# Where tiles live and who loads them: an earlier q, earlier half swaps and SyncE row loads in a planned kernel

## The chip, the cores and the metric

The kernel runs on one core of a Trainium2 chip. The metric is the device time of one execution in microseconds; the figure given is the median of five runs. A profile of one execution shows what each engine did: PE (TensorE matmuls, with PEld for its weight loads), DVE (VectorE), ACT (ScalarE), POOL (GpSimd, here the issuer of DMAs and little else) and SP (SyncE, which only issues DMAs).

## The reference, cut to what matters

Two independent branches share one output: columns 0 to 1023 are a long convolution, columns 1024 to 2047 a diagonal state-space recurrence. Sequence length S is 2048, width D is 1024, everything comes and goes as bf16.

```python
# branch A
k_shift = sum(k_pad[:, t:t+S, :] * shift_k[:, ks-1-t] for t in range(4))
kv = k_shift * v
y  = irfft(rfft(pad(kv, 2*S)) * rfft(pad(ssm_k, 2*S)))[:S]     # along S
a  = q * (y + kv * ssm_D)
# branch B
Bu = einsum("bld,pd->blp", x, B_bar)                           # complex
h[t] = Lam_bar * h[t-1] + Bu[:, t]                             # 2048 steps
b  = 2 * einsum("blp,dp->bld", h, C).real + x * Dskip
out = concatenate([a, b], -1)
```

## The kernel before

The whole work is one list of 1684 named steps, `ORDER`, written out by hand (or by a planner) in the source. Every step is a small function; each engine issues its own instructions in the order of the list, and semaphores between engines are put in automatically. A step that needs a tile buffer which an earlier tile still holds makes its first writer wait. So the list sets the order on each engine, and waits come from data, from buffers and from DMA landings.

**Branch B** works in 16 chunks i of 128 time steps.
- `xl`, `x`: load and transpose x. `bl.j.w` loads a tile of B (256 KB), `bT` transposes it on PE, `bc` copies it into `BT` (ACT for w = 0, DVE for w = 1). `cl`, `cT`, `cc`, `cx` do the same for C. `tab`, `sin`, `stt` and others build rotation tables.
- `U.i.p` (L468): 32 matmuls of 128 columns each, a quarter of x·B for chunk i; `ue.i.p` evicts on ACT.
- `r1`, `r2` (rotate and add, L480 and L489), `ca`, `sc` (two scans, L500), `cm`, `cy` (carry to the next chunk), `r3`, `r4`: the recurrence, all on DVE. Chunks follow each other through the carry.
- `y.i.h.part` (L524, L529): h·C and the skip term, on PE; `ye` evicts, `yst` stores; the last chunk is stored in halves by `ysh`.

**Branch A** does the FFT as three matmul stages with the data passed through DRAM.
- `k.r` and `v.n` load rows of k and v; `kvm`, `kva`, `kvb`, `kvc` (L569 to L587) make the shifted product on DVE for 16 row sets. `am` (PE), `ae` (ACT), `ast` (POOL) transform and store it to `Ys_kv`.
- `hl`, `hd`, `hT`, `hc`, `hm`, `he`, `hst` do the same for the filter, in four quarters, to `Ys_h`. This is the h stage; its tiles are `hT` and `ysbh`.
- The middle stage has 32 groups g, two in one load: `lh`, `l` load the filter's and the data's groups (512 KB each), `lw` the weights; `sh`, `sk` are matmuls (L674); `she` and `ske` evict to `hab` and `x16`. `sw.g` swaps the two halves of 64 partitions of `hab` with two DMAs from POOL (L701, L702), `pr.g` multiplies on DVE (L707), `sa` is the inverse matmul (L716), `sae` evicts and `vst` stores two groups to `Vs`.
- The last stage has 16 row sets n: `vl.n` loads two tiles `vv` from `Vs` (L734), `ql.n` a tile of q (L739), `a3` matmul (L746), `a3e` evict, `qm` multiply by q (L765), `ost` store; the last three row sets use `qp` and half stores `oth`.

Branch A's tiles of the stages live in three pools that follow each other in the same space: `a1` (rows and h stage), `a2` (the 32 groups), `a3` (last stage). The first tile of a pool closes the pool before:

```python
        if name not in pools:
            for o in list(cms):
                cms.pop(o).__exit__(None, None, None)
            cms[name] = tc.tile_pool(name=name, bufs=1)
```

So the first q tile, in `a3`, has to wait until every tile of `a2` that shares its space is free, the last `vsb` among them. `vv` has 7 buffers, `qt` 6, `hab` 4, `l2k` 3. The rows `k.-3` to `k.0` and `v.0` are loaded by POOL (`k.-3` to `k.-1` in two parts each, 112 and 15 rows), the other rows by SP.

Of the kernel before, what the change touches and what calls it, by code (L numbers as in the profile page):

```python
# [15 lines left out]
BF16 = mybir.dt.bfloat16  # L16
# [8 lines left out]
def a_constants():  # L25
# [12 lines left out]
    for si in range(4):  # L38
# [23 lines left out]
CFG = dict(nx=3, mt=2, u=3, xT=6, h=2, yo=2, ps_t=2, ps_u=2, ps_y=1, ps_a=3, kr=8, ld=5, acc=2, ysb=3, hk=3,  # L62
           hT=2, ysbh=2, l2=3, wts=4, swa=0, x16=4, hab=4, vsb=2, vv=7, qt=6, ot=5, bdve=8)
# [3 lines left out]
xl.0 xl.1 ld_F xl.2 bl.5.0 ld_par ld_w bl.1.1 bl.0.0 bl.3.0 k.-3 bl.0.1 bl.6.1 xt.0 k.-2 bl.1.0 bl.6.0 xt.1 x.0 bl.4.0  # L67
k.-1 bl.3.1 x.1 lw.0 par_T wb.0 bl.2.0 k.0 p32 bT.1.1 bl.4.1 ld_G exp1 bl.2.1 lw.1 v.0 wb.1 bc.1.1 bl.7.1 xt.2 wbe.0
hl.0.1 dve2 k.1 wbe.1 bT.5.0 dve3 x.2 tab.0 wb.4 bl.5.1 bc.5.0 bT.3.0 sm_pre x.4 exp2 wb.2 wbe.4 bT.0.1 bc.3.0 tab.1
lw.2 lw.3 dd wbe.2 x.3 bT.0.0 sin0 wb.3 wb.5 bc.0.1 wb.6 k.2 k.3 tab.2 bc.0.0 hl.0.0 bT.1.0 bc.1.0 par_rest bT.6.1  # L70
bl.7.0 wbe.6 U.0.0 x.5 wbe.3 wbe.5 tab.3 sin.2 bc.6.1 wb.7 U.1.0 hl.1.0 wbe.7 tab.4 k.4 z1.2 kvm.0 ue.0.0 bT.3.1
bT.6.0 sin.4 U.2.0 cl.0.1 ue.1.0 bc.3.1 z1.1 kva.0 bT.7.1 bc.6.0 bc.7.1 z1.0 bT.2.1 kvb.0 bT.4.0 ue.2.0 bc.2.1 bc.4.0
kvc.0 bT.4.1 eo.0 kvm.1 bT.2.0 v.2 am.0.0 v.1 am.0.1 am.0.2 bc.2.0 ae.0.2 U.0.1 bc.4.1 ae.0.0 eo.1 stt.0 am.0.3 ae.0.1
kvm.2 U.1.1 ae.0.3 ast.0.0 ue.0.1 ast.0.1 eo.2 bT.5.1 stt.1 U.2.1 cl.2.0 ue.1.1 k.5 bc.5.1 eo.3 bT.7.0 hd.0 kva.1
U.0.2 ue.2.1 cl.0.0 bc.7.0 stt.2 U.2.2 ue.0.2 kva.2 stt.3 U.0.3 ue.2.2 kvb.1 z2 kvb.2 cT.0.1 kvm.3 ue.0.3 U.1.2 cl.3.1
cc.0.1 cx.4.1 U.2.3 ue.1.2 kvc.1 cx.7.1 r1.0 cT.2.0 ue.2.3 U.1.3 cc.2.0 kvc.2 r2.0 cl.1.1 U.3.0 ue.1.3 cx.5.0 kva.3
k.6 cT.0.0 sc.0 ue.3.0 cl.1.0 am.1.0 U.3.1 cl.3.0 cc.0.0 cx.7.0 ae.1.0 am.1.1 cx.5.1 hT.0.0 ue.3.1 am.1.2 ae.1.1
am.1.3 U.3.2 hc.0.0 ast.1.0 k.7 v.3 ae.1.2 kvb.3 cx.4.0 ae.1.3 cm.0 cT.1.0 r3.0 ue.3.2 ast.1.1 cT.3.1 cc.1.0 am.2.0
am.2.1 cl.2.1 U.3.3 cc.3.1 kvm.4 ae.2.0 ae.2.1 cT.1.1 ue.3.3 hm.0.0.0 ast.2.0 am.2.2 v.4 cc.1.1 hT.0.1 v.5 r4.0
hm.0.0.1 he.0.0.0 he.0.0.1 kvc.3 hm.0.0.2 hT.0.2 ae.2.2 hst.0.0.0 r1.1 hc.0.1 hm.0.0.3 am.2.3 he.0.0.2 cT.3.0 he.0.0.3  # L80
v.8 cc.3.0 kva.4 hst.0.0.1 U.4.0 v.7 hc.0.2 r2.1 ae.2.3 U.4.1 ue.4.0 cy.0 ast.2.1 kvb.4 ca.1 kvm.5 cT.2.1 ue.4.1
hm.0.1.0 hT.0.3 cc.2.1 hm.0.1.1 hm.0.1.2 hl.1.1 U.4.2 he.0.1.0 kvm.6 cx.6.1 he.0.1.1 he.0.1.2 hst.0.1.0 cx.6.0
hm.0.1.3 y.0.0.0 ue.4.2 kvc.4 he.0.1.3 sc.1 am.3.0 hc.0.3 hl.2.0 U.4.3 hst.0.1.1 k.8 k.9 ae.3.0 v.6 v.9 am.3.1 y.0.0.1
ue.4.3 ae.3.1 hm.0.2.0 am.3.2 ast.3.0 hm.0.2.1 he.0.2.0 y.0.0.2 ae.3.2 kva.5 he.0.2.1 am.3.3 am.4.0 ae.3.3 am.4.1
hst.0.2.0 kva.6 y.0.0.3 ae.4.0 ae.4.1 hm.0.2.2 ye.0.0 cm.1 ast.3.1 kvb.5 he.0.2.2 ast.4.0 hd.1 r3.1 hT.1.0 hm.0.2.3
am.4.2 y.0.1.0 he.0.2.3 hc.1.0 hst.0.2.1 y.0.1.1 kvc.5 ae.4.2 r4.1 am.4.3 hT.1.1 x.6 ae.4.3 hm.0.3.0 y.0.1.2 kvb.6
he.0.3.0 ast.4.1 cy.1 r1.2 am.5.0 k.10 y.0.1.3 k.11 ae.5.0 v.12 hm.0.3.1 hT.1.2 ye.0.1 hm.0.3.2 he.0.3.1 hm.0.3.3
yst.0 kvc.6 he.0.3.2 U.5.0 hst.0.3.0 he.0.3.3 r2.2 hc.1.1 kvm.7 hst.0.3.1 U.5.1 ue.5.0 am.5.1 am.5.2 ue.5.1 ca.2 k.12
kva.7 hm.1.0.0 y.1.0.0 ae.5.2 ae.5.1 kvm.8 hT.1.3 ast.5.0 hm.1.0.1 he.1.0.0 U.5.2 hl.2.1 he.1.0.1 hst.1.0.0 sc.2 k.13
am.5.3 hl.3.0 hm.1.0.2 ue.5.2 hm.1.0.3 U.5.3 he.1.0.2 he.1.0.3 ae.5.3 hst.1.0.1 hc.1.2 y.1.0.1 ue.5.3 ast.5.1 am.6.0  # L90
y.1.0.2 ae.6.0 kvb.7 am.6.1 am.6.2 kva.8 hm.1.1.0 ae.6.1 ae.6.2 hm.1.1.1 ast.6.0 y.1.0.3 r3.2 he.1.1.0 he.1.1.1 am.6.3
hm.1.1.2 ye.1.0 hst.1.1.0 hm.1.1.3 ae.6.3 y.1.1.0 hc.1.3 kvc.7 ast.6.1 hm.1.2.0 cm.2 kvb.8 y.1.1.1 he.1.1.2 he.1.1.3
r4.2 am.7.0 hst.1.1.1 y.1.1.2 x.7 ae.7.0 hd.2 kvc.8 hT.2.0 y.1.1.3 r1.3 he.1.2.0 hT.2.1 ye.1.1 hm.1.2.1 hm.1.3.0
hm.1.3.1 he.1.2.1 yst.1 cy.2 kvm.9 U.6.0 hst.1.2.0 he.1.3.0 he.1.3.1 am.7.1 hst.1.3.0 U.6.1 ue.6.0 r2.3 k.14 ae.7.1
v.11 v.13 ast.7.0 kva.9 v.10 am.7.2 y.2.0.0 ue.6.1 ca.3 ae.7.2 kvm.10 hm.1.2.2 hm.1.2.3 y.2.0.1 he.1.2.2 he.1.2.3
U.6.2 hc.2.0 hst.1.2.1 sc.3 k.15 am.7.3 hm.1.3.2 ue.6.2 hm.1.3.3 y.2.0.2 ae.7.3 he.1.3.2 ast.7.1 U.6.3 hc.2.1 he.1.3.3
kvb.9 hst.1.3.1 am.8.0 am.8.1 ue.6.3 kva.10 hm.2.0.0 y.2.0.3 ae.8.0 ae.8.1 am.8.2 kvc.9 he.2.0.0 hT.2.2 ast.8.0 r3.3
ye.2.0 am.8.3 hm.2.0.1 ae.8.2 y.2.1.0 ae.8.3 he.2.0.1 ast.8.1 am.9.0 y.2.1.1 ae.9.0 cm.3 hst.2.0.0 kvb.10 am.9.1 r4.3
am.9.2 x.8 y.2.1.2 ae.9.1 ae.9.2 ast.9.0 kvc.10 hm.2.0.2 hm.2.0.3 hm.2.1.0 he.2.0.2 r1.4 y.2.1.3 he.2.0.3 hc.2.2
hT.2.3 hst.2.0.1 hm.2.1.1 hm.2.1.2 hl.3.1 ye.2.1 v.15 kvm.11 he.2.1.0 U.7.0 yst.2 he.2.1.1 hst.2.1.0 am.9.3 y.3.0.0  # L100
ue.7.0 r2.4 ae.9.3 y.3.0.1 he.2.1.2 ast.9.1 kva.11 hm.2.1.3 U.7.1 cy.3 hc.2.3 hd.3 ca.4 kvb.11 he.2.1.3 kvm.12 am.10.0
hst.2.1.1 am.10.1 ue.7.1 y.3.0.2 ae.10.0 ae.10.1 am.10.2 am.10.3 sc.4 hT.3.0 ae.10.2 ast.10.0 hm.2.2.0 ae.10.3
# [12 lines left out]
am.14.3 y.5.0.1 ae.14.2 ae.14.3 r2.6 am.15.3 U.9.0 ast.14.1 ae.15.3 lh.0 ast.15.1 lh.1 ca.6 sc.6 U.9.1 ue.9.0 U.9.2
ue.9.1 l.1 l.0 U.9.3 lh.2 ue.9.2 r3.6 l.2 y.5.0.2 ue.9.3 cm.6 sh.0.0 sh.0.1 r4.6 y.5.0.3 she.0.0 she.0.1 sh.1.0 cy.6
r1.7 sh.1.1 ye.5.0 sw.0 sh.2.0 lh.3 she.1.0 y.5.1.0 she.1.1 she.2.0 sw.1 sh.2.1 sh.3.0 she.2.1 U.10.0 she.3.0 sw.2
sk.2.0 sk.0.0 ue.10.0 y.5.1.1 ske.2.0 ske.0.0 sk.0.1 sk.1.0 x.11 y.5.1.2 ske.0.1 ske.1.0 pr.0 sk.1.1 sk.2.1 y.5.1.3
ske.1.1 ske.2.1 sa.0.0 ye.5.1 r2.7 sh.3.1 sa.0.1 sae.0.0 lh.4 yst.5 y.6.0.0 she.3.1 pr.1 sae.0.1 sw.3 sk.3.0 sk.3.1
y.6.0.1 ske.3.0 pr.2 l.3 ske.3.1 l.4 sa.1.0 ca.7 y.6.0.2 sc.7 sae.1.0 sh.4.0 sa.1.1 she.4.0 sk.4.0 y.6.0.3 sae.1.1  # L120
ske.4.0 lw.5 vst.0 sa.2.0 ye.6.0 sh.4.1 sk.4.1 sae.2.0 U.10.1 ske.4.1 she.4.1 pr.3 sw.4 sh.5.0 sh.5.1 ue.10.1 r3.7
y.6.1.0 lh.5 she.5.0 she.5.1 sa.2.1 sh.6.0 sw.5 sh.6.1 sae.2.1 y.6.1.1 cm.7 she.6.0 r4.7 she.6.1 sa.3.0 x.12 sk.5.0
# [53 lines left out]
def full_kernel(ctx, tc, A_q, A_k, A_v, A_shift_k, A_ssm_k, A_ssm_D, B_x, B_Lre, B_Lim, B_Bre, B_Bim,  # L176
                B_Cre, B_Cim, B_log_dt, B_Dskip, out, cfg=None):
    c = dict(CFG)
    c.update(cfg or {})
    nc = tc.nc  # L180
    P = 128
# [59 lines left out]
    def ap_pool(name):  # L241
        if name not in pools:
            for o in list(cms):
                cms.pop(o).__exit__(None, None, None)
            cms[name] = tc.tile_pool(name=name, bufs=1)
            pools[name] = cms[name].__enter__()
        return pools[name]
# [582 lines left out]
```

## Time and profile before

| | |
|---|---|
| median of five runs | 388.63 us (387.83 to 391.05) |
| the profiled execution's own time | 388.94 us |
| its span | 387.0 us |
| PE busy | 360.8 us |
| DVE busy | 329.5 us |
| ACT busy | 279.3 us |
| POOL busy | 128.2 us |
| DMA traffic | 101 MB, 261 GB/s on average |
| granted PE clock | 0.998 |

The span runs from the first to the last instruction; the execution's own time has 1.9 us more around it. Matmuls are pipelined, so PE's busy time says that PE had work in flight, not that it ran at its peak. [...] An engine's idle time counts only where that engine, or one that waits for it, sets the end.

### The profile page before, as it was taken

The page shows a single profiled execution, that of the slowest core. Times are in us where ns is not written, and L with a number is a line of the kernel's source. Part 1 is how long each engine was busy: PE and PEld are TensorE (multiplying, and loading weights), DVE is VectorE, ACT ScalarE, POOL GpSimd, SP SyncE. Part 2 cuts the span into 40 slices and gives each one's busy share as a digit, 9 for nine tenths or more (in the row PEclk, how much of TensorE's full clock was granted, in tenths as well). Part 3 has the DMA queues.
Part 4 walks back from the last instruction along what each step waited for, and adds up shares of the span by engine and source line. Part 5 has one row for each costly group of instructions (what it writes and reads, how often), then busy time and mean ns, then how long its engine had stood idle before and what let it go on. Part 6 is the DMA issues. An engine that isn't in the chain of part 4 may idle for free.

```text
span 387.0 us, 8963 instructions
## 1 busy us (share of the span) xinstructions
PE 360.8 (93%) x3509; PEld 246.9 (64%) x3553; DVE 329.5 (85%) x341; ACT 279.3 (72%) x511; POOL 128.2 (33%) x223
## 2 busy tenths in 40 slices
PE   3998998999999998999979999989998999999995
PEld 2687997859586775778536465555554676864442
DVE  2999999999999999999387999995853694989944
ACT  3799579787868698974857789868997876245331
POOL 7001003445555447661323234322343331011220
PEclk9999999999999999999999999999999999999999
DMA  7999399898685936456999999988999643998984
GB/s 241 367 311 336 103 229 338 237 314 282 260 243 192 286 125 217 191 174 211 287 263 262 331 262 305 281 299 269 319 276 276 234 152 135 319 402 278 371 314 164
DMA packets 60506, 101.15 MB, mean 261 GB/s; under 512 B 28451, under 2 KB 31523, under 8 KB 60464
## 3 DMA queue, kind: packets, MB, share of 16 engines
q1 hardware_dynamic: 46512, 58.21, 51.7%
q0 software_dynamic: 13872, 42.35, 30.2%
q8 instruction: 28, 0.46, 0.5%
q14 instruction: 14, 0.11, 0.1%
q10 hardware_dynamic: 80, 0.01, 0.0%
HBM read 53.10 MB, written 33.55 MB: 224 GB/s over the span
## 4 chain that ended last, share of the span: by engine, by line
PE 68%; DMA 12%; DVE 7%; issue 5%; ACT 5%; SPq 2%; POOL 0%; DVEq 0%; ACTq 0%
PE ps_u L468 23%; PE ps_y L524 22%; PE ps_a L716 6%; PE ps_a L674 5%; DMA hab<-hab 4%; DMA CT<-in_B_B_re_dram 4%; PE ps_a L746 3%; PE ps_a L593 2%; PE ps_a L639 2%; PE ps_y L529 2%; DVE mt L480 2%; PE ps_t L617 2%; DMA Ys_h<-ysbh 1%; DVE mt L569 1%; ACT ysbh L647 1%
## 5 line engine op out<-in xcount | busy, mean ns | idle before, releaser
L524 PE MATMUL ps_y<-CT,h 128*128 128x512 bf16 x478 | 130.1, 379 | 2.8 <-ACT yo L539 1.6
L468 PEld LDWEIGHTS <-BT 128*128 128x128 bf16 x2048 | 118.8, 98 | 8.7 <-ACT BT L434 1.3
L468 PE MATMUL ps_u<-xT,BT 128*128 128x128 bf16 x2048 | 123.3, 220 | 0.8 <-ACT BT L434 0.8
L524 PEld LDWEIGHTS <-h 128*128 128x128 bf16 x512 | 46.9, 98 | 47.0 <-issue 0.7
L500 DVE TENSOR_TENSOR_SCAN h<-rtab,h 128x1024 bf16<-128x1024 f32 x32 | 71.5, 2276 | 0.2
L470 ACT CAST u<-ps_u 128x512 bf16<-128x512 f32 x64 | 38.1, 595 | 41.2 <-PE ps_u L468 41.2
L707 DVE TENSOR_TENSOR hab<-x,hab 128x2048 bf16<-128x2048 bf16 x32 | 38.5, 1220 | 23.6 <-ACT vsb L727 11.5
L654 POOL DMA_DIRECT2D Ys_h<-ysbh x64 | 45.4, 713 | 33.5 <-ACT ysbh L647 33.2
L480 DVE TENSOR_TENSOR mt<-u,Z 128x4096 bf16<-128x4096 bf16 x16 | 36.6, 2286 | 10.6 <-ACT u L470 10.6
L727 ACT CAST vsb<-ps_a 128x512 bf16<-128x512 f32 x64 | 36.9, 599 | 10.8 <-PE ps_a L716 7.1
L647 ACT CAST ysbh<-ps_a 128x512 bf16<-128x512 f32 x64 | 36.5, 622 | 8.5 <-DMA Ys_h<-ysbh 5.9
L604 POOL DMA_DIRECT2D Ys_kv<-ysb x32 | 17.8, 557 | 64.8 <-ACT ysb L602 64.4
L602 ACT CAST ysb<-ps_a 128x512 bf16<-128x512 f32 x64 | 36.5, 616 | 3.6 <-PE ps_a L593 3.6
L696 ACT CAST x<-ps_a 128x512 bf16<-128x512 f32 x64 | 36.8, 597 | 3.1 <-PE ps_a L674 2.9
L716 PE MATMUL ps_a<-hab,wts 128*128 128x512 bf16 x122 | 34.8, 379 | 4.2 <-DVE hab L707 4.1
L684 ACT CAST hab<-ps_a 128x512 bf16<-128x512 f32 x64 | 36.4, 600 | 2.1 <-PE ps_a L674 1.9
L701 POOL DMA_DIRECT2D hab<-hab x32 | 16.9, 527 | 61.0 <-ACT hab L684 60.5
L480 DVE TENSOR_TENSOR mt<-h,Z 128x4096 bf16<-128x4096 bf16 x16 | 36.6, 2286 | 0.2
L569 DVE TENSOR_TENSOR mt<-kring,wbc 128x4096 bf16<-128x4096 bf16 (+3 forms) x16 | 30.1, 1883 | 0.0
L539 ACT CAST yo<-ps_y 128x512 bf16<-128x512 f32 x32 | 19.1, 598 | 15.1 <-PE ps_y L524 15.1
L529 PE MATMUL ps_y<-Dd,xT 128*128 128x128 bf16 x128 | 28.0, 219 | 0.6
L639 PE MATMUL ps_a<-hT,F1t 128*128 128x256 bf16 x128 | 21.7, 272 | 1.6 <-ACT ysb L602 0.8
(118 smaller groups left out, 459.0 us busy)
## 6 DMA issues: line engine op xcount, KB each, us to landing
Ys_kv<-ysb POOLq DMA_DIRECT2D x32, 256.0 KB, 3.2
Ys_h<-ysbh POOLq DMA_DIRECT2D x64, 128.0 KB, 3.3
hk<-Ys_h SPq DMA_DIRECT2D x16, 512.0 KB, 6.5
l2k<-Ys_kv SPq DMA_DIRECT2D x16, 512.0 KB, 5.6
hab<-hab POOLq DMA_DIRECT2D x64, 128.0 KB, 4.7
Vs<-vsb POOLq DMA_DIRECT2D x16, 512.0 KB, 5.4
vv<-Vs SPq DMA_DIRECT2D x32, 256.0 KB, 5.4
hk<-in_A_ssm_k_dram SPq DMA_DIRECT2D x8, 512.0 KB, 4.7
```

What stands on the lines that cost most here:

```text
L468: nc.tensor.matmul(pu[:, w, jl, :], BT[:, 2 * jp + jl, w, d, :], xT[:, d, :], start=(d == 0), stop=(d == ND - 1))
L470: E["ue"] = lambda i, jp: nc.scalar.copy(st["u", i][:, :, 2 * jp:2 * jp + 2, :], st.pop(("pu", i, jp))[:])
L480: nc.vector.tensor_mul(m, s_, win(Z))
L500: nc.vector.tensor_tensor_scan(gf[:, a * W:(a + 1) * W], rt1, gf[:, a * W:(a + 1) * W], 0.0, ALU.mult, ALU.add)
L524: nc.tensor.matmul(py[:], h[:, 1 - w, j, :], CT[:, j, w, dh * 512:(dh + 1) * 512], start=(j == 0 and w == 0), stop=(j == NJ - 1 and w == 1))
L602: nc.scalar.copy(st["ysb", n2, cc][:, dh * 512:(dh + 1) * 512], st.pop(("pa", n2, w))[:])
L647: nc.scalar.copy(st["yh", qd, n4, w // 2][:, :, w % 2, :], st.pop(("pa", qd, n4, w))[:].rearrange("p (c d) -> p c d", c=2))
L654: gpd(Ys_h[cc, n0:n0 + 2, :, qd * DQ:(qd + 1) * DQ].rearrange("n k d -> k n d"), t_[:, cc, :, :])
L696: nc.scalar.copy(st["x16", g][:, w * 512:(w + 1) * 512], st.pop(("ps", "l2k", g, w))[:])
L707: nc.vector.tensor_mul(hab[:], st.pop(("x16", g))[:].unsqueeze(1).to_broadcast([P, 2, D]), hab[:])
L716: nc.tensor.matmul(pt[:], st["w", gq][:, gi, 1 + a, :], hab[:, a, w * 512:(w + 1) * 512], start=(a == 0), stop=(a == 1))
L727: nc.scalar.copy(st["vsb", gq][:, gi, w * 512:(w + 1) * 512], st.pop(("ps", "v", g, w))[:])
```

## The change

All 1684 steps are kept, and their list is written anew in another order. The code differs in this:

```diff
-CFG = dict(nx=3, mt=2, u=3, ..., l2=3, ..., hab=4, vsb=2, vv=7, qt=6, ot=5, bdve=8)
+CFG = dict(nx=3, hb=2, mt=2, u=3, ..., l2=3, ..., hab=4, vsb=2, vv=5, qt=6, ot=5, bdve=8)
...
     def ap_pool(name):
         if name not in pools:
-            for o in list(cms):
-                cms.pop(o).__exit__(None, None, None)
-            cms[name] = tc.tile_pool(name=name, bufs=1)
+            if name == "a2k":
+                ap_pool("a2h")
+            dead = {"a2h": ("a1h",), "a2": ("a1",), "a2k": ("a1",), "a3q": ("a2k",), "a3": ("a2",)}.get(name, ())
+            for o in dead:
+                if o in cms:
+                    cms.pop(o).__exit__(None, None, None)
+            cms[name] = tc.tile_pool(name=name, bufs=1, side="left" if name in ("a1", "a2", "a3") else "right")
...
+    def kring():
+        if "kring" not in st:
+            st["kring"] = ap_pool("a1").tile([P, c["kr"], D], BF16, name="kring", bufs=1)
+            nc.vector.memset(st["kring"][0:1, 0:3, :], 0.0)
+        return st["kring"]
...
-        eng = spd if r > 0 else gpd
+        eng = spd
...
-        (spd if n2 else gpd)(st["v", n2][:], vr[:, n2, :])
+        spd(st["v", n2][:], vr[:, n2, :])
...
-        st["hT", qd, n4] = atile("a1", "hT", [P, 4, DQ])
+        st["hT", qd, n4] = atile("a1h", "hT", [P, 4, DQ])
...
-            st["yh", qd, n4, w // 2] = atile("a1", "ysbh", [P, 2, 2, DQ])
+            st["yh", qd, n4, w // 2] = atile("a1h", "ysbh", [P, 2, 2, DQ])
...
-            st[nm, gq] = ap_pool("a2").tile([P, GC, D], BF16, name=nm, bufs=c["l2"])
+            st[nm, gq] = ap_pool("a2k").tile([P, GC, D], BF16, name=nm, bufs=c["l2"])
...
-            st["hab", g] = atile("a2", "hab", [P, 2, D])
+            st["hab", g] = atile("a2h", "hb", [P, 2, D]) if g % 5 < c["hb"] else atile("a2", "hab", [P, 2, D])
...
-        st["qt", n2] = atile("a3", "qt", [P, D])
+        st["qt", n2] = atile("a3q", "qt", [P, D])
```

There are now two stacks of pools. On the left `a1`, `a2` and `a3` follow each other; on the right `a1h` (tiles of the h stage) gives way to `a2h`, two further buffers `hb` for `hab`, and `a2k` (the loaded data groups `l2k`) gives way to `a3q` (the q tiles). Two of five groups take `hb`, so `hab` and `hb` together have six buffers in place of four; `vv` has five in place of seven.

Three places of the new list that are spoken of below. The start, before:

```
xl.0 xl.1 ld_F xl.2 bl.5.0 ld_par ld_w bl.1.1 bl.0.0 bl.3.0 k.-3 bl.0.1 bl.6.1 xt.0 k.-2 bl.1.0 bl.6.0 xt.1 x.0 bl.4.0 k.-1 bl.3.1
```

and after:

```
xl.0 xl.1 ld_w xl.2 k.-3 ld_par bl.1.1 ld_F k.-2 ld_G bl.5.0 bl.1.0 xt.0 bl.0.1 k.-1 xt.1 x.0 bl.7.1 bl.0.0 wb.0 x.1 bl.2.0 par_T
wbe.0 bl.5.1 p32 bT.1.1 bl.3.0 exp1 bl.2.1 xt.2 bl.3.1 bc.1.1 bl.6.0 k.0 ...
```

The first groups, before:

```
lh.0 ast.15.1 lh.1 ca.6 sc.6 U.9.1 ue.9.0 U.9.2 ue.9.1 l.1 l.0 U.9.3 lh.2 ue.9.2 r3.6 l.2 y.5.0.2 ue.9.3 cm.6 sh.0.0 sh.0.1 r4.6
y.5.0.3 she.0.0 she.0.1 sh.1.0 cy.6 r1.7 sh.1.1 ye.5.0 sw.0 sh.2.0 lh.3 she.1.0 ...
```

and after:

```
lh.0 ast.15.1 lh.1 U.9.2 ue.9.1 y.5.0.2 ue.9.2 r3.6 y.5.0.3 l.0 l.1 U.9.3 ye.5.0 lh.2 cm.6 r4.6 y.5.1.0 ue.9.3 cy.6 r1.7 sh.0.0
sh.0.1 sh.1.0 she.0.0 y.5.1.1 she.0.1 she.1.0 sh.1.1 sw.0 sh.2.0 x.11 U.10.0 she.1.1 she.2.0 sw.1 l.2 ...
```

The end of the groups, after (before, the first `ql` and `vl` came behind the last `vst`):

```
ske.31.0 ql.1 U.13.3 ske.31.1 ql.4 pr.29 ql.5 sae.28.1 ql.0 ql.2 ql.6 pr.31 ... sa.31.1 sae.31.0 U.15.0 sae.31.1 r2.13 vst.15
ca.13 y.12.0.2 sc.13 ue.15.0 U.15.1 y.12.0.3 ue.15.1 U.15.2 vl.1 ye.12.0 vl.4 ...
```

## The prediction

> **What bounds the kernel now.** I read the page's engine line first, then busy time by stage, then the chain of waits, and last the single waits at the two pool changes.
>
> ```profile
> span 387.0 us, 8963 instructions
> ...
> PE 360.8 (93%) x3509; PEld 246.9 (64%) x3553; DVE 329.5 (85%) x341; ACT 279.3 (72%) x511; POOL 128.2 (33%) x223
> ```
>
> A busy PE of 93% overstates the work. In the timeline 32 matmuls of `U` take 1.79 us (56 ns each) and four of `y` take 0.86 us (215 ns each). At that pace all PE work (64 `U` pieces of 1.79, 512 `y` matmuls, and so on down the list of steps) adds up to 350.0 us, so 37 us of the span are lost on PE. Setting each step's measured start against the work ahead of it in the order gives where: 16.6 us before `U.0.1` at 32.0, 6.6 more until 155, then 3.0 at `sa.0.0`, 1.0 at `sa.4.0`, 1.3 at `sh.16.1`, 1.3 at `sa.23.0`, 2.1 in four places after 350, and 4.9 behind the last matmul at 382.1. The table by stage (columns PE, PEld, DVE, ACT, POOL) says which engine is the limit of each stage:
>
> ```profile
> 10.00:184.00 174.00, 166.94 (x1998) 132.69 (x2017) 172.43 (x205) 138.15 (x243) 65.94 (x101) 1.00 0.78 245
> 184.00:200.00 16.00, 13.31 (x90) 7.03 (x90) 8.18 (x9) 11.07 (x21) 4.75 (x9) 1.00 1.04 277
> 200.00:320.00 120.00, 116.44 (x914) 68.77 (x929) 97.75 (x78) 99.32 (x193) 40.35 (x76) 1.00 0.89 272
> 320.00:340.00 20.00, 19.89 (x263) 16.00 (x263) 13.85 (x12) 8.60 (x16) 1.08 (x2) 1.00 0.65 235
> 340.00:370.00 30.00, 28.86 (x168) 14.41 (x169) 28.80 (x26) 15.15 (x28) 5.43 (x10) 1.00 0.95 351
> ```
>
> From 10 to 184 **DVE** has 1.6 us of idle time in 174: whatever PE wins there it must give back, because `y` and `am` wait for DVE. From 184 to 340 **PE** is the limit. From 340 to 370 DVE is full again (the recurrence of the last two chunks). The largest single loss of the PE stage is the change of pools at 186:
>
> ```profile
> 184.63 2.20 DVE mt L480
> 186.84 7.59 issue
> 194.62 1.23 DVE hab L707
> 195.90 0.60 PE ps_a L716 x2
> ```
>
> The first product (L707) starts at 194.62, 7.6 us after DVE is free. The view of the tile `hab` between 184 and 200 shows what it waits for: the first swaps, issued at 185.6 and 186.2, are slow to land.
>
> ```profile
> DMA to landing us min/median/max: 7.4/8.2/8.8
> ```
>
> In the quiet stretch from 308 to 320 the same swaps land in 2.2 to 3.6 us. At the other pool change SyncE's queue waits long, but in the timeline PE doesn't: `q` is issued at 328.19, `Vs` rows at 331.13, and the first output matmul starts at 339.84 on time.
>
> ```profile
> SPq L739 <- DMA Vs<-vsb: 17.0, 2, 15.1
> ```
>
> **What the Trainium skill says.** "TensorE: Matmul & The Clock Gate", section "Wait — 56ns, not 53.3ns?", gives 55.6 and 215.7 ns start to start for 128 and 512 columns; the 56 and 215 ns above agree, so PE can't go faster per step. "DMA: Bandwidth & Descriptors", section "Issuing engines are not separate DMA queues", says that loads started by SyncE and GpSimd share the same 16 DMA engines. The trace agrees: swaps of GpSimd take 8.2 us beside SyncE's loads and 2.8 us (median) without. So moving `k`, `v` to SyncE brings no bandwidth, and a swap's price is the traffic beside it.
>
> **The change, part by part.** All 1684 steps stay the same; no arithmetic is added or removed. What changes is the order, who issues eight row loads, and which space tiles take.
>
> (a) *k, v rows on SyncE* (eight loads: six parts of `k.-3` to `k.-1`, `k.0`, `v.0`). POOL loses eight issues of about 0.55 us, that it had time for. SyncE gains eight: `bl.1.1` becomes its 6th load instead of the 5th, and `U.0.0` now stands behind `bT.3.1`, whose `bl.3.1` is the 20th load (before: `bl.1.0`, the 10th, was the last needed). The timeline of before for this place:
>
> ```profile
> 9.05 0.33 SPq L428 DMA_DIRECT2D CT<-in_B_B_im_dram  x1
> ...
> 17.27 0.33 SPq L608 DMA_DIRECT2D hk<-in_A_ssm_k_dram  x1
> ...
> 22.85 2.29 DVE L569 TENSOR_TENSOR mt<-kring,wbc 128x4096 bf16<-128x4096 bf16 x1
> ```
>
> Lower bound by bytes: up to `bl.3.1` 4.4 MB pass (3 x, 3 k, 11 B tiles, the small constants); at the page's 241 and 367 GB/s for the first two slices that is 15.3 us. I take 18, since SyncE's 20th load went out at 17.27 before with up to 3 MB in flight and now has no POOL loads beside it. The limit is DVE: it reaches this place (`bc.6.1` then, `bc.3.1` now) at 21.05, so a `bl.3.1` at 18 (transpose and copy 1.7) is in time, and the first `kvm` stays at 22.85. Cost 0; kept for the range: from -0.5 (DVE starts its first copy earlier) to +6 (below). `r1.0` comes 4.5 us earlier on DVE, but only because a `kvm`, a `kva` and two small ones go behind it; the DVE work ahead of `r1.6` is 151.7 before and 151.6 after, ahead of `r1.7` 163.1 both. With DVE full, that stage ends when it did: **0**.
>
> (b) *Early swaps in h-stage space*. The first swap still follows `she.0.1`, and PE work between `sh.0.1` and `sa.0.0` grows only from 8.9 to 9.2 us. Needed at the old landing: 11.8. What changes is the traffic: before, four loads of 512 KB went out from 183.1 to 184.4 ahead of the first swap and `lh.3` with it (2.6 MB; at the 277 GB/s of that stage 9.4 us). Now three are ahead (`l.0`, `l.1`, `lh.2`), then the `x.11` transpose; `l.2` comes after the second swap, `lh.3` far later: about 2.0 MB. Scaled, 8.2 x 2.0/2.6 = 6.3 us to landing, 9.9 needed, 9.2 covered: a stall of 0.7 to 0.9 in place of 3.0. **-2.1**; bounds -3.0 (no stall) and -0.4 (old landing).
>
> (c) *The groups after that*. With the old landings, I set the PE work from `sh.g.1` to `sa.g.0` against what each group needed (to its swap's landing, and 1.3 for the product). `sa.23.0`: 9.1 becomes 10.6 against 10.3 needed, so its 1.3 goes. `sa.4.0`: 10.9 becomes 10.1, so its 1.0 becomes 1.7 (its product stands behind `r1.8` on DVE either way). Group 6: 11.6 becomes 9.3 against 10.3: +0.3 beside the stall of group 4. `sh.16.1` keeps its neighbours. Two more buffers for `hab` let swaps run ahead but shorten no chain. **-0.2**; bounds -3.3 (all stalls gone) and +2.
>
> (d) *q early, five vv buffers*. `q` needs nobody's wait on PE, so its earlier start saves nothing by itself. It is needed, though: `sae.31.1` moves 3.6 us back in PE's work while the first `a3` stays (309.8 before, 308.9 now), leaving 10.8 us of PE work between. Before, 3.5 us passed from the end of `sae.31.1` (324.7) to the first issue that waits for its store, and five `q` issues (2.9 us) stood ahead of `vl`; without these the chain is 3.5 + 1.5 (four `vv` issues) + 5.4 (their median landing) = 10.4: just hidden. If that cover fails, the first `a3` is late by the difference. Later `vl` have short covers (5.4 to 6.8 us for 2, 3, 8, 10, 14 against about 0.9 of issue and the 4.8 to 5.5 that loads take there). The end is set by DVE from `U.14.3` to `r4.15`: `U.14.3` ends 2.3 us later in PE's work, then 1.2 us less DVE work (28.0 for 29.2) and 1.3 less PE work after `y.15.0.0`: together **-0.2**; bounds -1.5 and +4 (a late `vl` holds `qm` on DVE, and `r3.15` stands behind it).
>
> (e) *Tail*. Four of the eight last stores went out after the last matmul, 0.5 us apart; now `ysh.0` goes out earlier, so three: **-0.5**.
>
> Sum: 0 - 2.1 - 0.2 - 0.2 - 0.5 = -3.0. The profiled execution has a span of 387.0 and its own time is 388.94, 0.3 over the median of 388.63; so the span would be 384.0, that execution's time 385.9, the median **385.6**.
>
> **Rivals.** *Nothing is gained at the pool change*: the swap lands as late as before and other groups stall a little more; speaks for it that `sh.0.1` to `sa.0.0` grew by 0.3 only. 388 us, chance 0.20. *More is gained*: six `hab` buffers and lighter DMA take the stalls of (c) too, 388.63 - 6 = 382.6; against it, the covers of groups 4, 6 and 8 shrink. 0.12. *Slower: SyncE's start queue.* Its loads take completion semaphores in turn, and six k loads now stand among the B tiles. If the queue keeps the old pace per load, the 20th goes out at 17.27 and lands after the 8.85 us that one issued at 9.05 took: 26.1. Then transpose 1.03, `bc.3.1` 0.69, `tab.4` 1.22: `kvm` at 29.1, 6.3 late, and full DVE never gives it back: 385.6 + 6.3 = 391.9. It makes the kernel slower overall from a landing at 22.8 on. Against it: three of the six have only 15 rows, and POOL's 1.1 MB beside them are gone. 0.13. *Slower at the end*: the short `vl` covers cost 4 on DVE's chain, and group stalls 1: 390.6. 0.10.
>
> **Numbers.** Forecast case 0.45, median 385.6. Over 0.5% (1.9 us, about what a measurement of this kernel can tell from no change) faster is below 386.7: the forecast and the greater gain, 0.57, less a little for its upper edge: 0.55. Within: 0.22. Slower: 0.23, the two slow cases. Range 381.5 (the bounds of b and c together) to 392.0 (the slow start).
>
> **What would show it.** Right: first `kvm` at 22 to 24; DVE still full from 10 to 184; the first product before 193.5 with swap landings near 6 us; no PE wait before the first `a3`; `q` issued before the last `vst`. Wrong: `kvm` after 24 (a); swaps again over 8 us (b); new waits of PE on L707 in groups 4 to 8 (c); DVE idle ahead of L765 or L480 after 345 (d).

## The result, and the profile after

The change makes the kernel faster by about 0.6%: the median is **386.12 us** (42 executions, 383.66 to 394.27) against 388.83 us (79 executions, 385.01 to 394.36), ratio 0.9937 with a 95% interval of 0.9922 to 0.9952. Here and below, medians are over all executions of a kernel, while the ratios leave out its slow ones, so a ratio is not quite the quotient of the medians beside it. The profiled execution took 385.96 us, its span is 384.0. In the profile after, line numbers are 10 higher than before from `U` on (L468 is now L478, L707 is L717, and so on). First the page's engine line, then the table by stage (PE, PEld, DVE, ACT, POOL, granted clock, DMA share, GB/s), for the same stretches as before:

```profile
span 384.0 us, 8964 instructions
...
PE 360.2 (94%) x3508; PEld 246.2 (64%) x3553; DVE 330.3 (86%) x341; ACT 278.8 (73%) x511; POOL 125.0 (33%) x215
```

```profile
10.00:184.00 174.00, 166.53 (x1997) 131.64 (x2015) 173.07 (x207) 138.27 (x243) 66.90 (x101) 1.00 0.82 245
184.00:200.00 16.00, 15.23 (x110) 8.35 (x110) 7.78 (x6) 12.12 (x24) 4.75 (x9) 1.00 0.97 274
200.00:320.00 120.00, 117.65 (x940) 69.98 (x953) 99.00 (x81) 99.31 (x194) 40.40 (x76) 1.00 0.91 271
320.00:340.00 20.00, 18.29 (x227) 14.00 (x227) 13.32 (x11) 8.70 (x16) 1.08 (x2) 1.00 0.78 273
340.00:370.00 30.00, 28.49 (x171) 14.44 (x173) 28.51 (x26) 15.02 (x28) 7.06 (x13) 1.00 0.94 317
```

Read the PE column downwards. Between 184 and 200 PE works 15.2 of 16 us (before 13.3): that is the gain. Between 320 and 340 it works 18.3 of 20 (before 19.9): there something is lost. DVE is full from 10 to 184 as before (173.1 of 174). The two places are named by the landing line of the tile `hb` (the early `hab` buffers; 184 to 200) and by PE's waits from 186 to 340, first before, then after:

```profile
DMA to landing us min/median/max: 5.6/6.9/8.3
```

```profile
PE ps_a L716 <- DVE hab L707: 4.1, 3, 2.6
PE ps_a L674 <- ACT vsb L727: 1.1, 1, 1.1
```

```profile
PE ps_a L726 <- DVE hab L717: 1.2, 1, 1.2
PE ps_a L756 <- DMA vv<-Vs: 1.1, 1, 1.1
PE ps_a L726 <- DVE hb L717: 0.6, 1, 0.6
PE ps_a L726 <- ACT vsb L737: 0.5, 1, 0.5
PE ps_a L684 <- ACT vsb L737: 0.3, 1, 0.3
```

The wait for the first product (L717 on `hb`) is down from 2.6 to 0.6 us. Two waits are new. In the first line `sa.2.0` waits for the product of group 2, which before came in time (see (c) below). In the second an `a3` matmul waits for `vv`. SyncE's DMA queue shows what holds up the loads of `vv`: they wait for the landing of the last `Vs` stores. Behind that line stand the landings of the last two of these stores (320 to 340), first before, then after:

```profile
SPq L744 <- DMA Vs<-vsb: 9.7, 3, 7.5
```

```profile
DMA to landing us min/median/max: 2.9/2.9/2.9
```

```profile
DMA to landing us min/median/max: 6.3/7.0/7.6
```

`q` indeed goes out early, from 317.98 to 320.59. But the first `vl` still waits for the last `Vs` store and goes out at 331.03 (before 331.13).

An account of the losses makes the two executions comparable. A step's **loss** is its start minus the PE work ahead of it in the list (350.0 us in all, both kernels). The loss of a stretch is what this grows by from its first step to its last, so the losses add up to span minus 350. The second execution of the changed kernel is e12 below.

| stretch | before | after | after, e12 | change | predicted |
|---|---|---|---|---|---|
| start to `sh.0.0` | 23.1 | 22.4 | 22.6 | -0.7, -0.5 | 0 |
| `sh.0.0` to `sa.0.0` | 3.2 | 1.2 | 1.6 | -2.0, -1.6 | -2.1 |
| `sa.0.0` to `sh.31.1` | 3.5 | 2.3 | 3.3 | -1.2, -0.2 | -0.2 |
| `sh.31.1` to `U.14.3` | 0.3 | 2.0 | 2.0 | +1.7, +1.7 | -0.2 with the next |
| `U.14.3` to the last matmul | 1.95 | 1.7 | 1.7 | -0.3, -0.3 | |
| after the last matmul | 5.0 | 4.3 | 4.3 | -0.7, -0.7 | -0.5 |
| sum | 37.0 | 34.0 | 35.5 | -3.0, -1.5 | -3.0 |

### The profile page after: what moved, and what is told of

The parts are those of the page before. It is cut to its first block, busy times and chain, and to the rows that moved or that the text cites. A ratio compares the mean times of both kernels' runs of the same rounds, so it can differ in the third digit from the quotient of the medians.

```text
span 384.0 us, 8964 instructions
## 1 busy us (share of the span) xinstructions
PE 360.2 (94%) x3508; PEld 246.2 (64%) x3553; DVE 330.3 (86%) x341; ACT 278.8 (73%) x511; POOL 125.0 (33%) x215
## 4 chain that ended last, share of the span: by engine, by line
PE 71%; DVE 12%; DMA 9%; issue 3%; ACT 2%; SPq 1%; POOL 1%; ACTq 0%; DVEq 0%; POOLq 0%
PE ps_u L478 23%; PE ps_y L534 22%; PE ps_a L684 6%; PE ps_a L726 6%; PE ps_a L756 4%; DVE h L510 3%; PE ps_t L430 3%; PE ps_a L603 2%; DMA hb<-hb 2%; DVE mt L579 2%; PE ps_a L649 2%; DMA Ys_h<-ysbh 2%; PE ps_y L539 2%; DVE mt L586 1%; DMA vv<-Vs 1%
## 5 line engine op out<-in xcount | busy, mean ns | idle before, releaser
L478 PEld LDWEIGHTS <-BT 128*128 128x128 bf16 x2048 | 118.9, 98 | 8.9 <-issue 1.0
L478 PE MATMUL ps_u<-xT,BT 128*128 128x128 bf16 x2048 | 123.9, 219 | 0.1
L737 ACT CAST vsb<-ps_a 128x512 bf16<-128x512 f32 x64 | 36.0, 599 | 8.8 <-PE ps_a L726 7.2
L717 DVE TENSOR_TENSOR hab<-x,hab 128x2048 bf16<-128x2048 bf16 x18 | 21.9, 1218 | 12.3 <-DMA hab<-hab 11.5
L717 DVE TENSOR_TENSOR hb<-x,hb 128x2048 bf16<-128x2048 bf16 x14 | 17.0, 1223 | 10.7 <-DMA hb<-hb 7.1
L499 DVE TENSOR_TENSOR h<-mt 128x2048 bf16<-128x2048 bf16 x16 | 19.5, 1220 | 5.9 <-PE ps_y L534 5.7
L649 PE MATMUL ps_a<-hT,F1t 128*128 128x256 bf16 x128 | 22.6, 272 | 1.5 <-ACT ysb L612 0.6
L603 PE MATMUL ps_a<-acc,F1t 128*128 128x512 bf16 x60 | 20.7, 379 | 2.3 <-ACT ysbh L657 2.1
```

The lines of the kernel that those rows point to most:

```text
L478: nc.tensor.matmul(pu[:, w, jl, :], BT[:, 2 * jp + jl, w, d, :], xT[:, d, :], start=(d == 0), stop=(d == ND - 1))
L717: nc.vector.tensor_mul(hab[:], st.pop(("x16", g))[:].unsqueeze(1).to_broadcast([P, 2, D]), hab[:])
L737: nc.scalar.copy(st["vsb", gq][:, gi, w * 512:(w + 1) * 512], st.pop(("ps", "v", g, w))[:])
```

## The experiments

The **theory** after the comparison: the gain at the pool change is DMA traffic taken away from beside the first swaps, not space; the rows on SyncE are worth nothing; the early `q` loads slow the last `Vs` stores and cost what shows between `sh.31.1` and `U.14.3`. The **rivals**: the two buffers in h-stage space make the gain; the rows make it; the early `q` helps. Ratios are to before, with 95% intervals. A single execution differs from another of the same kernel by several us, so verdicts on time rest on ratios, and the traces serve for the mechanism.

### The pool change: traffic or space

**e2**, from after:
```diff
-l.0 l.1 U.9.3 ye.5.0 lh.2 cm.6 ... sw.0 sh.2.0 x.11 ... sw.1 l.2 ... ske.1.0 lh.3 pr.0
+l.0 l.1 U.9.3 ye.5.0 lh.2 l.2 cm.6 ... sw.0 lh.3 sh.2.0 x.11 ... sw.1 ... ske.1.0 pr.0
```


> The kernel after with two loads of 512 KB moved back to where before had them: l.2 behind lh.2, ahead of the first swap, and lh.3 right behind sw.0. Buffers, pools and all else stay. My theory, that the stall at the pool change is set by the DMA traffic beside the first swaps: their landing goes back from 5.6-6.5 to about 8 us, the stall at sa.0.0 from 1.0 to 2.0-3.0, the time up by 1 to 2 us (ratio to before 0.996 to 0.999). Rival, that the space of hab (the two buffers in h-stage space) made the gain: no change, stall 1.0, ratio 0.993 to 0.995.

Measured: 387.68 us, ratio 0.9993 (0.9967 to 1.0019), a little above the range of the theory; loss up to `sa.0.0` 2.6 in place of 1.2, and 1.3 more up to `sa.1.0`, where PE ran at half its clock (last section). The landing of `hb` (184 to 196) and PE's wait for the first product:

```profile
DMA to landing us min/median/max: 7.4/8.2/9.2
```

```profile
PE ps_a L726 <- DVE hb L717: 2.1, 1, 2.1
```

With the two loads back, landings are those of before (7.4/8.2/8.8), although `hb` lies in h-stage space. No gain is left that can be measured.

**e4**, from after:
```diff
-CFG = dict(nx=3, hb=2, ..., hab=4, ...)
+CFG = dict(nx=3, hb=0, ..., hab=6, ...)
```


> The kernel after with all six hab buffers in the pool a2, none in the space of the h stage; the order of the steps is that of after. My theory: the swaps go out when she.0.1 is done, in either space, since the tiles of a1 are free by then; first swap, stall at sa.0.0 (1.0) and span (384.0) within 0.7 us of after, ratio to before 0.993 to 0.996. Rival, that the h-stage space lets hab be written earlier: she.0.0 waits, the first swap goes out 1 to 2 us later, the stall is 2 to 3 us, ratio 0.996 to 1.0.

Measured: 386.58 us, ratio 0.992 (0.9894 to 0.9946), span 383.5; first swap issued at 187.13 (after 186.81), landed in 6.2 and 7.1 us, loss up to `sa.0.0` 1.8. The ratio is a little below the expected range and its interval holds that of after, so the place of the buffers isn't the gain. The 0.6 us more of loss lies within what one execution differs by.

**e8**, from before:
```diff
-r3.6 l.2 y.5.0.2 ... sh.2.0 lh.3 she.1.0 ... sw.1 sh.2.1 ... ske.1.0 pr.0
+r3.6 y.5.0.2 ... sh.2.0 she.1.0 ... sw.1 l.2 sh.2.1 ... ske.1.0 lh.3 pr.0
```


> The kernel before with one part of the change alone: l.2 moved behind sw.1 and lh.3 behind ske.1.0, so that two loads of 512 KB no longer stand ahead of the first swaps. No new pool, no new buffer. My theory, that traffic sets the stall at the pool change: first swap lands in about 6 us instead of 7.5 to 8.2, the stall at sa.0.0 falls from 3.0 to about 1, and the time by 1 to 2 us, ratio 0.994 to 0.998. Rival, that it takes h-stage space or the other order of steps: the landing stays near 8, ratio 0.999 to 1.001. A new wait for the later l.2 or lh.3 would show as a stall at sk.4.0 or sh.6.0.

Measured: 389.01 us, ratio 0.999 (0.9969 to 1.0011); landing of the first swap 6.9 and 7.5 us, loss up to `sa.0.0` 2.5 in place of 3.2. A miss, and an instructive one: `l.2` still went out at 184.22, ahead of the swaps. Nothing on SyncE's own queue stood in its way, so moving `l.2` behind a step of POOL in the list moved it past nothing. Only `lh.3` was taken away.

**e9**, from before, with `l.2` behind `x.11`, a transpose that SyncE itself issues, at 192.50 in this trace:
```diff
-r3.6 l.2 y.5.0.2 ... sh.2.0 lh.3 she.1.0 ... x.11 y.5.1.2 ... ske.1.0 pr.0
+r3.6 y.5.0.2 ... sh.2.0 she.1.0 ... x.11 l.2 y.5.1.2 ... ske.1.0 lh.3 pr.0
```


> The kernel before with l.2 put behind x.11 in the list, so that SyncE, which takes its instructions in order, can't issue it ahead of the first swaps (in e8 it still did, at 184.2), and lh.3 behind ske.1.0. Then 1.5 MB of loads are ahead of the first swap instead of 2.6. My theory, that the traffic sets the stall at the pool change: first swaps land in 5 to 6 us (before 7.5 and 8.2), the stall at sa.0.0 falls from 3.0 to 0.5-1.3, ratio 0.994 to 0.998. Rival, that the time comes from elsewhere (or a late l.2 makes sk.4.0 wait for as much as was won): ratio 0.999 or above.

Measured: 387.19 us, ratio **0.9958** (0.9934 to 0.9983): 1.6 us, from the order of two loads alone. Loss up to `sa.0.0` 1.3 in place of 3.2. The first swap took 6.4 and 6.3 us, a little over the 5 to 6 expected. The landing of `hab` between 184 and 200, in before 7.4/8.2/8.8:

```profile
DMA to landing us min/median/max: 5.3/6.0/7.7
```

By the medians this is more than half of what the whole change gains, with none of its buffers or pools.

**e10**, from e7 (below):
```diff
-ye.5.0 lh.2 cm.6 ... sh.2.0 x.11 U.10.0
+ye.5.0 cm.6 ... sh.2.0 x.11 lh.2 U.10.0
```


> The kernel of e7 with lh.2 behind x.11 as well, so that only l.0 and l.1 (1.0 MB) are ahead of the first swap. My theory: first swaps land in 4 to 5 us, no stall at sa.0.0 (e7: 1.2), the next swaps (sw.1, sw.2) keep 7 to 8 us since lh.2 and l.2 now go beside them, and sa.2.0 keeps its 1.5; the time 0.5 to 1 us below e7, ratio 0.988 to 0.993. Rival, that the stall only moves from sa.0.0 to sa.1.0 or sa.2.0, or to sh.4.0 that needs lh.2: time as e7 or above, ratio 0.992 or above.

Measured: **384.0 us**, ratio 0.9887 (0.9842 to 0.9931), span 382.8; e7 had 0.9921 (0.9889 to 0.9952). Landing of `hb` (184 to 196), and all that PE waits for from 186 to 340:

```profile
DMA to landing us min/median/max: 3.9/5.2/6.3
```

```profile
PE ps_a L684 <- ACT vsb L737: 1.6, 2, 1.3
```

The wait for the first product is gone (first swap 3.95 and 4.8 us), and `sa.2.0`, expected to keep its 1.5, loses 0.4. But the loss from `sa.0.0` to `sh.31.1` is 3.2 against e7's 2.3: PE loses 1.5 us around `sh.8.0` and `U.11.0`, behind evictions to `vsb`. Both the theory and the rival are half right. e10 has the lowest median and is faster than before; its interval still touches that of after, so that it beats after too isn't shown.

### The last stage: what the early q does

**e3**, from after:
```diff
-ske.31.0 ql.1 U.13.3 ske.31.1 ql.4 pr.29 ql.5 sae.28.1 ql.0 ql.2 ql.6 pr.31 ... vl.6 cm.13
+ske.31.0 U.13.3 ske.31.1 pr.29 sae.28.1 pr.31 ... vl.6 ql.1 ql.4 ql.5 ql.0 ql.2 ql.6 cm.13
```


> The kernel after with its six early q loads (ql.1, 4, 5, 0, 2, 6) moved behind vl.6, all else as it is. My theory, that they sit beside the last Vs stores and delay the vl loads that wait for these: vst.15 lands in about 3 us instead of 6.3, the first vl goes out at about 328 instead of 331, the waits of PE at U.15.0, a3.1.0 and y.15.0.0 shrink by 1 to 2 us together, span 382 to 383, ratio to before 0.988 to 0.992. Rival, that the early q is what helps the end (or that q now comes too late for qm): no change or slower than after, ratio 0.994 or above.

Measured: 387.05 us, ratio 0.9953 (0.9927 to 0.998), span 384.2. The mechanism came as expected: the last store lands in 3.96 us (6.29), the first `vl` goes out at 329.12, the first `a3` doesn't wait. The time did not. DVE's timeline shows what is late next (start, duration, instruction, idle time before it):

```profile
340.79 0.69 DVE L775 TENSOR_TENSOR ot<-ot,qt 128x1024 bf16<-128x1024 bf16 x1 [6.78 <-DMA qt<-in_A_q_dram]
341.39 2.28 DVE L490 TENSOR_TENSOR mt<-u,Z 128x4096 bf16<-128x4096 bf16 x1
```

`qm.1` waits for its q tile, and `r1.14` behind it starts at 341.39, though its `U.14.3` ended at 339.42 and a start 0.8 later was possible.

**e7**, e3 with one more move:
```diff
-a3e.1.1 qm.1 ql.3 ost.1 a3.4.1 ... a3e.4.1 r1.14 y.12.1.3
+a3e.1.1 ql.3 a3.4.1 ... a3e.4.1 r1.14 qm.1 ost.1 y.12.1.3
```


> The kernel of e3 (all six q loads behind vl.6) with qm.1 and ost.1 moved behind r1.14, so that a late q.1 can't hold r1.14 on the vector engine. My theory, that e3 lost there what it won at the first a3 (r1.14 at 341.39 though its U.14.3 ended at 339.4): r1.14 at 339.5 to 340.3, y.15.0.0 at 368 to 369, ratio to before 0.988 to 0.993. Rival, that r1.14 isn't the limit, and later q or vv loads set the end: r4.15 still ends at 369 or later, ratio 0.994 or above.

Measured: 385.45 us, ratio 0.9921 (0.9889 to 0.9952), span 382.7. Here are `r1.14`, now ahead of `qm.1`, and the landing of the last two `Vs` stores:

```profile
339.27 2.29 DVE L490 TENSOR_TENSOR mt<-u,Z 128x4096 bf16<-128x4096 bf16 x1 [6.24 <-ACT u L480]
```

```profile
DMA to landing us min/median/max: 2.9/3.5/4.0
```

`r1.14` is 1.8 us earlier than in after, PE waits for nothing between 320 and 340, `r4.15` ends at 368.26 (after 369.55), and the loss from `sh.31.1` to `U.14.3` is 0.2 in place of 2.0. Against the two executions of after that is a gain of 1.8. It is not what the early q loads cost in general: e1, e2 and e4 keep all six of them in their place, and lose 0.2, 0.6 and 0.7 there (see e12). In the ratio the difference to after is too small to be told apart, and e3, which moves the loads alone, isn't faster than after either.

**e6**, from after:
```diff
-ql.4 pr.29 ql.5 sae.28.1 ql.0 ql.2 ql.6 pr.31 ... vl.6 cm.13
+ql.4 pr.29 sae.28.1 pr.31 ... vl.6 ql.5 ql.0 ql.2 ql.6 cm.13
```


> The kernel after with only ql.1 and ql.4 loaded early; ql.5, 0, 2 and 6 go behind vl.6. My theory, that the 1.5 MB of six q loads beside the last Vs stores delay these, while q.1 and q.4 are the only ones that are needed before 345: the last Vs store lands in 4 to 5 us, the first vl goes out at about 329.5, no wait at a3.1.0, qm.1 no longer waits for its q tile, r1.14 starts at 339.5 to 340.5 (after: 341.07), span 382 to 383, ratio to before 0.987 to 0.992. Rival, that two q loads are enough to delay the stores, or that the end is not set there: r1.14 at 341 or later, ratio 0.993 or above.

Measured: 386.34 us, ratio 0.9921 (0.9891 to 0.995), span 384.7. The last store lands in 4.0 us, `a3.1.0` doesn't wait and `qm.1` has its q tile. But the last store was issued only at 326.47 (after 324.59), since this execution was 1.9 us behind by `sae.31.1`, so the first `vl` went out at 330.63 and `r1.14` at 341.70. The loss from `sh.31.1` to `U.14.3` is 0.8. By `r1.14` the rival is right, by the ratio the theory, and the interval holds that of after: the run decides nothing.

**e5**, from after, with the early q undone as a whole:
```diff
-st["qt", n2] = atile("a3q", "qt", [P, D])
+st["qt", n2] = atile("a3", "qt", [P, D])
...
-ske.31.0 ql.1 U.13.3 ske.31.1 ql.4 pr.29 ql.5 sae.28.1 ql.0 ql.2 ql.6 pr.31 ... vl.1
+ske.31.0 U.13.3 ske.31.1 pr.29 sae.28.1 pr.31 ... ql.1 ql.4 ql.5 ql.0 ql.2 ql.6 vl.1
```
(The pool `a3` then also waits for `a2k`.)


> The kernel after with the early q undone as a whole: q tiles come from the pool a3 as in before, so they wait for the last vsb tiles, and the six q loads stand ahead of vl.1 again. All else is that of after. My theory, that q early as it stands has no worth because what it clears from the queue it loses in the last Vs stores: these land in about 3 to 4 us instead of 6 to 8, q goes out at about 328, the first vl at 331 (after: 331.03), the first a3 wait about as in after; ratio to before 0.992 to 0.996. Rival, that q early gives a part of the gain: first vl at 332 or later, the time 1 us or more above after, ratio 0.997 or above.

Measured: **391.91 us**, ratio 1.0055 (1.0022 to 1.0088), slower than before. My theory was wrong on this run, and the rival right by more than it asked for. PE's timeline, and the stretch 340 to 346 (PE, PEld, DVE, ACT, POOL, granted clock):

```profile
340.41 2.81 PE L756 MATMUL ps_a<-vv,Gt 128*128 128x512 bf16 x6 [3.32 <-DMA vv<-Vs]
343.01 3.58 PE L478 MATMUL ps_u<-xT,BT 128*128 128x128 bf16 x32
```

```profile
340.00:346.00 6.00, 5.59 (x34) 3.81 (x35) 0.69 (x1) 1.75 (x3) 0.55 (x1) 0.50 0.77 284
```

Six q loads ahead of `vl` put its first issue at 332.64 and its first landings at 338.5 and 340.3, PE waits 3.3 us, and then runs at half its clock: 32 matmuls of `U` take 3.58 us instead of 1.8. `r1.14` comes at 347.25, 6.2 us later than in after. In before this order of loads did no harm, since 15.2 us passed on PE between the end of `sae.31.1` and `a3.1.0`; in the new list it is 11.9 where nothing waits between them (e3). So the new list needs q out of `vl`'s way; early is one place for it, behind `vl.6` is another.

### Who loads the rows

**e1**, from after (**e11**: the same edit on e7):
```diff
-        eng = spd
+        eng = spd if r > 0 else gpd
...
-    spd(st["v", n2][:], vr[:, n2, :])
+    (spd if n2 else gpd)(st["v", n2][:], vr[:, n2, :])
```


> The kernel after with k.-3 to k.0 and v.0 loaded by GpSimd again, nothing else changed. My theory: who loads these rows is worth next to nothing (the first kvm was at 22.85 before and 22.30 after, DVE full from there to 184). So first kvm 22 to 24, r1.7 at 183.9 to 184.8, span within 0.7 us of the 384.0 of after, ratio to before 0.993 to 0.996. Rival: the rows on SyncE are the gain, or are a loss paid back elsewhere: then the time moves by 2 us or more, ratio 0.998 or above (or below 0.990).

> The kernel of e7 with k.-3 to k.0 and v.0 loaded by GpSimd again, as in e1. e1 had a ratio of 0.990 with an interval that just reaches that of after, while its profile showed no gain. My theory, that who loads these rows is worth nothing: ratio within 0.002 of that of e7 (0.992), first kvm at 21.5 to 23. Rival, that SyncE's rows cost something at the start: ratio 0.987 to 0.990.

Measured: e1 385.7 us, ratio 0.9902 (0.9872 to 0.9932); e11 385.38 us, ratio 0.9917 (0.9889 to 0.9946) beside e7's 0.9921. First `kvm` at 22.5 and 22.2. Rows on SyncE are no gain; e1 alone would allow a small cost, e11 doesn't bear it out. In both traces the front end is later (`r1.7` at 186.2 and 186.6, after 183.9), and e1's expectation of 183.9 to 184.8 was missed. In e1 PE waited 4.2 us for a tile of B and its clock was granted at 0.74 from 10 to 30; in e11, whose profiled execution took 3.7 us more than its median, DVE was busy only 17.4 of the same 20 us at a clock of 1.00. Since the medians don't show it, whether the rows have a part in it stays open.

### The changed kernel again

**e12** is after without an edit.


> The kernel after, unchanged, beside e10 and e11 on the same chip, so that a version made from it is compared with it there and so that its own spread is seen. Expected: ratio 0.992 to 0.996, the last Vs stores again at 6 to 8 us, the first vl at 331, waits of PE of 0.5 to 1.3 us at U.15.0 or a3.1.0. If these waits are gone in this execution, they were chance, and what e3 and e7 won is not shown.

Measured: 385.37 us, ratio 0.9931 (0.9906 to 0.9956), span 385.5. The last store lands in 5.87 us, the first `vl` goes out at 331.86, PE waits at `U.15.0` and loses 1.4 at `a3.1.0`. The loss is there in both executions, and of the same size (2.0).

But three more traces have the same list from `ql.1` to the end: e1, e2 and e4. In them nothing waits at `a3.1.0`, and the loss from `sh.31.1` to `U.14.3` is 0.2, 0.6 and 0.7. So the loss of 2.0 doesn't belong to the list alone. What differs is how late the last store lands, and the traffic shows how that comes about. This is the DMA rate while the last store of after is in flight (324.59 to 330.89, 40 slices), with one line of its queues:

```profile
GB/s 390 429 468 442 442 416 416 416 416 390 442 403 429 416 416 416 416 260 104 130 26 26 0 0 0 26 0 0 26 0 26 26 26 26 26 26 26 0 0 0
q8 instruction: 1, 0.02, 1.0%
```

After 3.2 us the bulk is through; then only single packets of 4 KB run, one behind the other (26 GB/s is one in a slice of 0.16 us). Just there the queue that the view calls `instruction` has one packet of 16 KB, which took 1.0 us, and the store's last packets come behind it. The packet's start, counted from the issue of the last store, sorts all fourteen traces into groups (us):

| runs | early q loads | packet starts after | last store lands after |
|---|---|---|---|
| before, e8, e9 | none | no packet | 2.9 |
| e3, e5, e7, e10, e11 | none | 0.5 to 0.7 | 3.8 to 4.05 |
| e6 | two | 0.4 | 4.0 |
| e1, e2, e4 | six | 1.1 to 1.6 | 4.5 to 4.8 |
| after, e12 | six | 3.1, 2.8 | 6.3, 5.9 |

With a packet, the landing comes 3.0 to 3.8 us behind its start in every trace. The early q loads may act through it, since with six of them the packet comes later. No run moves the packet alone, so how the delay is shared between the two isn't shown.

## Why the prediction came out as it did, step by step

The total was nearly met (386.12 for 385.6), but not each term. That the span of this execution fell by just the 3.0 predicted is luck: (d) missed by +1.6, and the stretches of (a) and (c) by -0.7 and -1.0.

(a) *Rows on SyncE*, **right**: 0 was predicted, the first `kvm` came at 22.30 (22 to 24), DVE stayed full, e1 and e11 show no worth either way.

(b) *Pool change*, **right in mechanism and size**: -2.1 predicted, -2.0 and -1.6 measured, first swap 5.6 and 6.5 us (6.3 predicted), stall 1.0 and 1.35 (0.7 to 0.9 predicted). e2, e9 and e10 confirm the step "what changes is the traffic". One sign failed by a little: the first product started at 194.15, not before 193.5. A part of this gain is lost again at group 2 (c): up to `sa.4.0` the loss shrinks from 4.0 to 2.6 and 3.1, in e9 with the old order to 2.2.

(c) *Later groups*, **right in sum, within what one execution tells, but not in its parts**: -0.2 predicted, -1.2 in one trace and -0.2 in the other. Executions with this middle order, e1 to e7 and e11 among them, lose 2.2 to 3.7 us here; the three of before's order lose 3.0 to 3.5. The single pair of traces would have misled: the wait at `sh.16.1`, which the prediction kept, was gone in after, but also in e8 and e9, where the order there is that of before. That wait was for a `Vs` store that took 7.55 us in that one execution. `sa.4.0` was to lose 1.7 and loses 0.2 in both executions. Instead `sa.2.0` loses 1.5 in both, and nothing in before; the prediction has no term for it. Its product `pr.2` stood ahead of the two scans `sc.7` on DVE, and in the new list stands behind them. The 1.3 at `sa.23.0` is gone in after, but 1.1 of it is there in e12. DVE's timeline, first before, then after:

```profile
196.90 2.35 DVE L707 TENSOR_TENSOR hab<-x,hab 128x2048 bf16<-128x2048 bf16 x2
199.42 4.47 DVE L500 TENSOR_TENSOR_SCAN h<-rtab,h 128x1024 bf16<-128x1024 f32 x2
```

```profile
198.23 4.47 DVE L510 TENSOR_TENSOR_SCAN h<-rtab,h 128x1024 bf16<-128x1024 f32 x2
202.62 1.20 DVE L717 TENSOR_TENSOR hab<-x,hab 128x2048 bf16<-128x2048 bf16 x1
```

(d) *q early*, **wrong in its steps, and in its sum for the two executions of after**. The step "the chain is 3.5 + 1.5 + 5.4 = 10.4: just hidden" failed in its first term: from the end of `sae.31.1` (324.30) to the first `vl` (331.03) passed 6.7 us, not 3.5, in e12 6.3, because the last store landed late (6.3 and 5.9 for 2.9). I had put the early q at no cost, without asking what it flies beside; (b) priced just that for the swaps. In e1, e2 and e4 the term was 5.0 to 5.3 and the chain just hidden, as predicted. With q late (e3, e7, e10, e11) it was 4.2 to 4.5, still not 3.5. So the term was mis-sized in every trace of the new order, by 0.7 to 3.2 us; how much of that is the q loads and how much the instruction packet isn't separated (e12). The second failure is "1.2 less DVE work": from `r1.14` to the end of `r4.15` pass 28.5 us in both kernels, DVE nearly full in both, with eight `qm` in before's stretch and nine in after's. What made up for it was missing from the prediction. In before the first matmul of `y.15` stood behind an eviction that frees its bank, in after it follows `r4.15` (ends 369.20 and 369.55) at once; first before, then after:

```profile
370.66 0.38 PE L524 MATMUL ps_y<-CT,h 128*128 128x512 bf16 x1 [0.67 <-ACT yo L539]
```

```profile
369.61 0.39 PE L534 MATMUL ps_y<-CT,h 128*128 128x512 bf16 x1 [0.62 <-ACT ot L764]
```

That is 1.46 us behind `r4.15` before and 0.06 after: -1.4. With the 1.3 less PE work behind it (11.4 to 10.1 us, as predicted) and no gain on DVE, (d) measures +1.7 - 0.3 = +1.4 in after and e12 instead of -0.2. In e1, e2 and e4 the same two stretches give -0.4, +0.1 and +0.2. That this meets the -0.2 is luck too: the DVE work that didn't shrink and the eviction that was left out cancel.

(e) *Tail*, **right**: -0.5 predicted, -0.7 measured; two stores, not three, go out after the last matmul.

Of the signs named: `q` went out before the last `vst` (right), no PE wait before the first `a3` matmuls (wrong: 0.6 at `U.15.0`, 1.25 at `a3.1.0`). The rival with a slower end had the right place, the `vl` chain, but that chain cost 1.7 at most and not 4 to 5. No new wait came up in groups 4 to 8, as the prediction feared, but one in group 2. e5 shows what the `vl` chain costs where q isn't out of the way.

## What to carry to other kernels

Ask of every load that is moved what lands beside it: two loads of half a megabyte cost 1.6 to 2.2 us of the kernel's time where a swap that someone waits for is in flight (e9, e2). A load can be held back only by an instruction that its own queue waits at, so move it behind such a one and check the issue time in the trace (e8, e9). Before calling a wait removed or added, compare several executions with the same list in that stretch. Here two agreed to the tenth on a loss of 2.0, and three others had 0.2 to 0.7.

## What the runs showed of the hardware

- **A swap's landing follows the loads ahead of it.** The first swap took 7.5 and 8.2 us with four loads of 512 KB ahead and a fifth beside it (before), 6.9 and 7.5 with four (e8), 6.4 and 6.3 with three (e9), 5.6 and 6.5 with three and a transpose (after), 3.95 and 4.8 with two and a transpose (e10). "DMA: Bandwidth & Descriptors" of the Trainium skill, section "Issuing engines are not separate DMA queues", says that loads of SyncE and GpSimd share the same 16 DMA engines; these rows agree, POOL's swaps slow down with SyncE's loads.
- **A store that meets a packet of instructions lands late.** Without one beside it the last `Vs` store of 512 KB landed in 2.9 us; with one of 16 KB, which took 0.9 to 1.7 us, in 3.8 to 6.3, and always 3.0 to 3.8 us behind the packet's start (table under e12). That the packet is the cause fits all fourteen traces, but no run moves it alone.
- **A wait of PE can cost twice.** In e5 a wait of 3.3 us was followed by a granted clock of 0.50 until 346; in e2 one of 2.05 us and in e11 one of 2.24 us were followed by this, while in before one of 2.61 us left the clock at 1.00. From e2:

```profile
198.00:199.00 1.00, 1.00 (x3) 0.30 (x2) 0.97 (x3) 0.12 (x1) 0.00 (x0) 0.50 1.15 180
199.00:200.00 1.00, 1.00 (x4) 0.38 (x3) 1.00 (x1) 0.96 (x2) 0.00 (x0) 0.50 1.00 209
```

  "TensorE: Matmul & The Clock Gate" of the Trainium skill, section "Part 1: The HAM clock gate (the "warmup" mystery)", tells of a free-running window of about 3.4 us of idleness. The half clock lasted 3.4 us in e2 (197.35 to 200.77) and in e11, and 6.8 in e5, once and twice the page's figure, so the length agrees. The waits of 2.05 and 2.24 us that set it off are shorter than the page's idle window, and there the measurement stands. That a longer wait in before didn't set it off would fit a window that runs freely; no run here tests that.
